# Attention LayerNorm rows of tiles 14 to 31 transposed on VectorE and by DMA, with channel blocks innermost, on one Trainium2 core

## The chip, the core and the metric

The kernel runs on one core of one Trainium2 chip. The core has TensorE (PE, matrix products into PSUM; its weight loads are shown as PEld), VectorE (DVE), ScalarE (ACT), GpSimd (POOL) and SyncE (SP, which issues all DMAs here). The metric is the device time in microseconds, the median of several runs. Before the change it is 463.86 us (three runs, 463.34 to 464.38).

## What is computed

A sequence of 2048 rows with 512 channels passes twice through an attention layer and an MLP layer with the same weights. Each has a LayerNorm ahead of it and a residual behind it. Attention has 32 heads of 16 channels and a sliding window of 256 rows.

```python
def _A_ref(x, wqkv, wo):
    B, S, D = x.shape
    H = 32; Dh = D // H; W = 256
    qkv = (x @ wqkv).reshape(B, S, 3, H, Dh).transpose(2, 0, 3, 1, 4)
    q, k, v = qkv[0], qkv[1], qkv[2]
    scores = jnp.einsum("bhqd,bhkd->bhqk", q, k) * (Dh ** -0.5)
    idx = jnp.arange(S)
    mask = (idx[:, None] - idx[None, :] >= 0) & (idx[:, None] - idx[None, :] < W)
    scores = jnp.where(mask[None, None], scores, -1e9)
    p = _softmax(scores, axis=-1)
    o = jnp.einsum("bhqk,bhkd->bhqd", p, v)
    return o.transpose(0, 2, 1, 3).reshape(B, S, D) @ wo

def _B_ref(x, w1, b1, w2, b2):
    h = _gelu(jnp.einsum("bsd,df->bsf", x, w1) + b1)     # 512 -> 1792
    return jnp.einsum("bsf,fd->bsd", h, w2) + b2         # 1792 -> 512

x = A_x
x = x + _A_ref(_layernorm(x, axis=-1), A_wqkv, A_wo)
x = x + _B_ref(_layernorm(x, axis=-1), B_w1, B_b1, B_w2, B_b2)
x = x + _A_ref(_layernorm(x, axis=-1), A_wqkv, A_wo)
x = x + _B_ref(_layernorm(x, axis=-1), B_w1, B_b1, B_w2, B_b2)
```

## The kernel before

Rows are worked on in tiles of 128. The two passes have 16 tiles each and are numbered through as tiles (tau) 0 to 31, so attention tile 16 reads the rows that MLP tile 0 of the first pass wrote. Two tiles make an attention batch, 16 batches in all. X, all weights and every intermediate stay in SBUF; input and weights are loaded in the first 40 us, and the only other traffic is the scratch transposes described below and the output.

For a batch b, `lnq(b)` normalizes two tiles (`layernorm`, layer 0), brings them channel-major into `xnTA[:, b % 2]` and projects Q from it; `kv(b)` projects K and V from the same buffer (`proj`, `pe_group`). Q and K use `xnTA` as the moving operand, 256 columns in each of the four channel chunks dc; V uses it as the stationary operand, 128 columns per tile and chunk. `xnTA` has two buffers, so batch b+2 can be written only when Q, K and V of batch b have read it. `attention(b)` then makes score visits (24 or 16 small matmuls into four PSUM banks, an exponential of ScalarE for each two banks, line 1111, and 0/1 masks on VectorE or GpSimd, line 1132), the product with V into two banks (PV), and the division, transposed on VectorE (lines 1197 to 1207). `outproj` adds the output projection to X (`residual`, line 990), and `layernorm(tau, 1, ...)` prepares the MLP's operand `xnTB`. `mlp(J)` runs jobs of two or four tiles: W1, GELU on ScalarE into `gT`, W2, residual.

`layernorm` has statistics and normalization on VectorE and GpSimd (lines 933 to 943), which give `xn`, rows in partitions. Then there are two ways to put channels in partitions. The first: four 128x128 transposes on TensorE into one PSUM bank (line 36 is the helper that records them) and one copy out of PSUM by VectorE (line 916) or ScalarE (line 918). The second, taken where `by_dma(tau, layer)` holds: VectorE transposes each 32x32 block within its 32 partitions (line 952, into the buffer `xs_`), four DMAs write one 32-row group each into the scratch `scr` in HBM (line 956), and one DMA reads it back with 1 KB in each partition (line 960). Before the change this second way is taken by MLP tiles 4 to 29 and by no attention tile.

PSUM has eight banks. A group takes banks from the first free entry of its class's list: "sc" four banks for a visit, "od" two for PV, "o" and "m1" one. The class "o" holds Q, K, V, output projection, W2, the first six W1 groups of a job and the transposes; its list is banks 6 and 7.

All instructions are added as nodes with what they read and write. The sequence on every engine is a written-out list of node numbers, `ORDER`; a negative entry ~i means node i on its second engine (a copy on ScalarE for VectorE, a mask or a product on GpSimd). `_Plan.follow` walks the list and assigns banks by estimated times; each engine then runs its part of the list strictly in order, with semaphore waits where data or buffers require them. SyncE's queue is one such sequence: a DMA whose data or target are not ready holds up the DMAs behind it.

Of the kernel before, what the change touches and what calls it, by code (L numbers as in the profile page):

```python
# [6 lines left out]
dt = mybir.dt  # L7
# [511 lines left out]
def bass_interleave_layers__sliding_block__dense_activation_gelu__prompt_kernel(  # L519
# [11 lines left out]
    Bb, S, D = A_x.shape  # L531
    assert Bb == 1
    P = 128
# [28 lines left out]
    NXS = 3  # L562
    NSC = 4

    def by_dma(tau, layer):
        return layer and 4 <= tau < NT - 2
# [26 lines left out]
    with ExitStack() as kctx:  # L593
        S_ = _Sched(nc, kctx)

        def sb(name, shape, dtype=dt.bfloat16):
# [21 lines left out]
        scr = nc.dram_tensor("scr_x", (NSC, 4, 32, 4, P), dt.bfloat16, kind="Internal").ap()  # L618
        xnTA = sb("xnTA", [P, 2, DC, 2 * P])
# [16 lines left out]
            3, 0, 8, 9, 10, 4, 5, 6, 7, 18, 19, 20, 21, 22, 15, 23, 33, 24, 40, 34, 41, 1, 11, 12, 13, 14, 2, 35, 36,  # L636
            42, 43, 84, 85, 86, 37, 44, 16, 17, 38, -40, 77, 45, -47, 87, 88, 89, -91, 57, 58, 59, 47, 60, 78, 79, 80,
            81, 82, -84, 48, 49, 52, 50, -52, 25, 91, 92, 93, 94, -96, 26, 53, 54, 55, -57, 72, 61, 154, 155, 156, 96,
            62, 63, 64, 67, 65, 68, 69, 70, 97, -72, 145, 146, 98, 99, 73, 74, 75, -101, 236, 101, 237, 108, 102, 103,
            229, 109, 110, 104, 105, 111, 66, 358, 359, 238, 230, 360, 361, 76, 135, 136, 137, 112, 231, 138, 139, 147,  # L640
            -149, 232, 239, 365, 28, 158, 159, 27, 140, 141, 142, 106, 107, 143, -145, 29, 30, 149, 150, 151, -158,
            -154, 815, 31, 32, 366, 367, 113, 114, 587, 594, 125, 126, 127, 160, 115, 116, 117, 118, 119, 163, 164,
            165, 128, 129, 120, 121, 122, 123, 124, 183, 184, 185, 253, 254, 255, 130, 256, 131, 240, 166, 233, 257,
            187, 189, 188, -162, -153, -163, 368, 132, 133, 134, 234, 235, 588, 951, 178, 180, 179, 263, 264, 241, 242,
            265, 266, 267, 192, 194, 193, 362, 369, 595, 243, 244, 245, 246, 247, -192, 958, 167, 182, 190, 248, 249,
            250, 251, -253, 168, 169, 170, 959, 589, 258, 259, 260, 261, 262, 172, 268, 269, 270, 271, -273, -197, 186,
            181, 173, 174, 363, -365, 286, 287, 288, 590, -172, 370, 371, 175, 273, 274, 275, 195, 197, 198, 176, 822,
            177, 291, 292, 293, 372, 373, 374, 375, -291, -277, 199, 200, -202, 378, 277, 278, 279, -295, -296, 376,
            377, 379, 380, 381, 382, 202, 383, 282, 284, 283, 384, 385, 386, 387, 823, 388, 816, -281, 216, 311, 313,
            312, 217, 218, 219, 203, 204, 205, 206, 281, 289, 220, 315, 316, 317, -286, 300, 207, 596, 208, 209, 210,  # L650
            296, 298, 297, 221, 222, 211, 212, 223, 301, 302, 320, 321, 322, 213, 224, 225, 226, 404, 406, 405, 214,
            817, 227, 430, 960, 431, 416, 417, 591, 299, 303, 432, -320, -326, 961, 215, 418, 306, 308, 307, 413, 414,
            415, 420, 421, 422, 389, 408, 410, 409, 427, 428, 429, 419, 433, 439, 440, 464, 465, 466, 467, 468, 441,
            390, 434, 435, 436, 437, 391, 423, 424, 392, 309, 318, 310, 314, 323, 326, 425, 426, 324, 411, 438, 469,
            470, 471, 327, 472, 473, 393, -305, 328, 454, 444, 459, 460, 461, 462, 442, 455, 456, 597, 598, 329, 330,
            331, 463, 443, 445, 446, 447, 448, 457, 458, 449, 450, 399, 451, 452, 453, 518, 400, 401, 519, 520, 402,
            403, 394, 395, 396, 397, 398, 952, 489, 490, 491, 492, 305, 824, 592, 593, 504, 505, 506, 493, 494, 332,
            333, 334, 335, 336, 337, 338, 495, -413, 228, 825, -408, -522, 339, 340, 508, 509, 496, 497, 345, 346, 347,
            348, 349, 350, 507, 513, 351, 352, 510, -512, 515, 514, -517, 353, 498, 499, 500, 501, 502, 503, 1216, 474,
            533, 535, 534, 475, 476, 477, 478, 479, 480, 528, 530, 529, 599, 600, 341, 354, 1217, 512, 517, 1218, 481,  # L660
            482, 483, 484, 485, 953, 342, 343, -537, -532, 537, 538, 539, -542, -541, 818, 486, 487, 488, 1209, 522,
            355, -357, 523, 524, 542, 543, 544, -547, -546, 671, 672, 673, 657, 658, 659, 525, 640, 642, 641, 664, 665,
            666, 668, 669, 670, 654, 644, 646, 645, 655, 1210, 656, 601, 602, 603, 604, 605, 532, 826, 526, 1211, 819,
            527, 661, 635, 636, -648, 637, -640, 662, 663, 606, 607, 547, 608, 609, -611, 548, 549, 550, 649, 650, 651,
            616, 617, 618, 619, 620, 611, 612, 631, 632, 613, 614, 615, 667, 680, 681, 682, 683, 684, 690, 691, 675,
            676, 692, 705, 693, 694, 677, 678, 679, 674, 685, 686, 687, 688, 689, 706, 707, 708, 709, -552, 552, 570,
            571, 572, 573, 574, 575, -649, -644, 357, -654, 954, 1212, 344, 700, 701, 660, 702, 703, 704, 553, 554,
            555, 556, 557, 558, 559, 560, 576, 577, 561, -653, 621, 710, 695, 696, 697, 698, 699, 711, 712, 622, 713,
            714, 623, 624, 625, 626, 627, 628, 629, 630, 764, 578, 820, 821, 715, 716, 827, 717, 828, 718, 719, 720,
            829, 830, 831, 633, 638, 955, 634, 562, 563, 567, 566, 962, 579, 580, 581, 583, 582, 564, 565, 584, 585,  # L670
            568, 766, 765, -770, 755, 756, 757, -760, 749, 750, 751, 752, 753, 754, 832, -834, 770, 772, 771, -775,
            -774, 721, 722, 723, 724, 725, 726, 745, 746, 747, 834, 835, 836, 837, 838, 727, 728, 729, 1345, 748, 758,
            760, 762, 761, 763, 767, 730, 731, 732, 733, 734, 863, 1219, 586, -769, 735, 736, 737, 738, 739, 775, 776,
            777, 778, -780, 864, 865, -868, 877, 878, 879, -882, 849, 740, 850, 741, 742, 743, 744, 868, 869, 870,
            -872, 851, 852, 853, 780, 839, 840, 841, 842, 843, 859, 861, 860, -867, -863, 844, 845, 846, 847, 848, 901,
            902, 903, -906, 854, 855, 856, 857, 858, 781, 782, 783, 784, 785, 786, 872, 874, 798, 799, 800, 801, 802,
            787, 956, 957, 873, 876, 875, 788, 892, 894, 893, 975, 976, 963, 964, 1346, 880, 803, 789, 804, 805, 790,
            791, 793, 794, 792, 977, 978, 897, 899, 898, 965, 966, 882, 884, 883, 967, 886, 968, -970, 887, 806, 807,
            808, 795, 810, 812, 809, 811, 896, 979, -905, 797, -901, -896, -886, 1004, 1006, 1005, 888, 1352, 889, 970,
            995, 996, 997, 980, 981, 982, 983, 906, 907, 908, 984, 910, 909, 1353, 971, 972, 973, -975, 1008, 1010,  # L680
            1009, 796, 813, 1043, 1044, 1045, 1213, 890, 891, 911, 1046, 1047, 1048, 999, 1001, 1000, -1003, -1004,
            1060, 1061, 1062, 1050, 912, 913, 1033, 1035, 1034, 1051, 1052, 914, -916, -1012, 985, 986, 987, 988, 989,
            1018, 1020, 1019, -1008, -1013, 990, 991, 992, 993, 994, 1053, 1013, 1014, 1015, -999, 916, 1054, 1055,
            1233, 1234, 1235, 1236, 1237, 1028, 1030, 1029, 917, 918, 919, 920, 921, 922, 1354, 1220, 1016, 934, 935,
            936, 1017, 1038, 1040, 1039, 1057, 1058, 1059, 1056, 1094, 1049, 1095, 1096, 1022, 1097, 1098, 1063, -1033,
            923, 924, 925, 926, 927, 937, 938, 939, 1021, 1037, 1031, 940, 941, 1214, 1215, 1064, 1099, 1100, 1023,
            1065, 1069, 1070, 1074, 1066, 1067, 1068, 1075, 1076, 1077, 1078, 942, 569, 1024, 1025, -1027, 1347, 1348,
            1027, 943, 944, 945, 930, 947, 948, 946, 949, 1071, 1072, 1073, 1101, 1102, 1089, 1079, 1080, 1090, 1081,
            1091, 1103, 1082, 1083, 1092, 1084, 1085, 1093, 1086, 1087, 1088, 1266, 1268, 1355, -1043, 1267, -1271,
            933, 814, 1104, 1105, 1106, 1149, 1150, 1107, 1108, 1109, 1151, 1152, 1153, 1154, 1155, 1253, 1254, 1255,  # L690
# [302 lines left out]
        def lnq(b, prio, pair=(0, 0)):  # L993

            xs = b % 2
            for j in range(2):
                layernorm(2 * b + j, 0, xnTA[:, xs, :, j * P : (j + 1) * P].rearrange("p c (r j) -> p r c j", r=4), "xa%d_%d" % (xs, j),
                          prio + (60 * j if b < 2 else 0))
# [360 lines left out]
```

## Time and profile before

| What | us |
|---|---|
| median of three runs | 463.86 |
| the profiled execution | 463.21 |
| its span, first to last instruction | 461.5 |
| TensorE busy | 435.0 |
| ScalarE busy | 393.2 |
| VectorE busy | 353.9 |
| GpSimd busy | 266.2 |
| Q and K matmuls (128x256, 512 of them), mean of one | 0.277 |
| one TensorE transpose, mean of one | 0.220 |

The granted TensorE clock is 0.996 of full speed. Durations of matmuls include their latency, which the next matmul overlaps; where it matters, the distance between the starts of two matmuls is used. DMA engines are busy for 13.5% of the span on average, most of it in the first 40 us. In lines of the profile, "out<-in" names what is written and read, and the numbers after the bar are busy time, mean duration in ns, and the idle time before those instructions with what ended it.

### The profile page before, as it was taken

The page shows a single profiled execution, that of the slowest core. Times are in us where ns is not written, and L with a number is a line of the kernel's source. Part 1 is how long each engine was busy: PE and PEld are TensorE (multiplying, and loading weights), DVE is VectorE, ACT ScalarE, POOL GpSimd, SP SyncE. Part 2 cuts the span into 40 slices and gives each one's busy share as a digit, 9 for nine tenths or more (in the row PEclk, how much of TensorE's full clock was granted, in tenths as well). Part 3 has the DMA queues.
Part 4 walks back from the last instruction along what each step waited for, and adds up shares of the span by engine and source line. Part 5 has one row for each costly group of instructions (what it writes and reads, how often), then busy time and mean ns, then how long its engine had stood idle before and what let it go on. Part 6 is the DMA issues. An engine that isn't in the chain of part 4 may idle for free.

```text
span 461.5 us, 19303 instructions
## 1 busy us (share of the span) xinstructions
PE 435.0 (94%) x8723; PEld 235.2 (51%) x8793; DVE 353.9 (77%) x699; ACT 393.2 (85%) x474; POOL 266.2 (58%) x302
## 2 busy tenths in 40 slices
PE   7997799999879999999999999999999999999997
PEld 3554464654444455555445545555454554454663
DVE  5998887887978679886998789885877867586402
ACT  3998999998999979898997999979988899873342
POOL 4367446776647466784629677595527535763210
PEclk9998999999999999999999999999999999999999
DMA  7570000002020011102010012101010111002101
GB/s 228 194 277 4 4 3 3 4 6 46 3 48 3 14 26 18 46 7 44 15 37 4 4 20 46 31 12 38 6 45 14 31 43 41 21 6 58 58 11 59
DMA packets 27857, 18.18 MB, mean 39 GB/s; under 512 B 15869, under 2 KB 27261, under 8 KB 27773
## 3 DMA queue, kind: packets, MB, share of 16 engines
q1 hardware_dynamic: 27772, 16.92, 13.5%
q8 instruction: 69, 1.13, 1.0%
q14 instruction: 16, 0.12, 0.1%
HBM read 11.41 MB, written 5.51 MB: 37 GB/s over the span
## 4 chain that ended last, share of the span: by engine, by line
PE 71%; ACT 16%; DVE 6%; DMA 2%; issue 2%; POOL 1%; SPq 1%; DVEq 0%; POOLq 0%
PE ps L32 69%; ACT E L1111 12%; PE ps L36 2%; SPq L956 1%; ACT gT L1278 1%; DMA scr_x<-xs_ 1%; DMA xnTB<-scr_x 1%; POOL E L1132 1%; DVE X L990 1%; ACT gT L1269 1%; DVE gT L1266 1%; DVE stat L933 1%; DVE xs_ L952 1%; ACT L1111 1%; ACT L1269 1%
## 5 line engine op out<-in xcount | busy, mean ns | idle before, releaser
L1111 ACT ACTIVATE E<-ps 128x1024 bf16<-128x1024 f32 x304 | 286.6, 1051 | 25.9 <-PE ps L32 25.1
L1132 POOL TENSOR_TENSOR E<-E,mask 128x512 bf16<-128x512 bf16 (+1 forms) x170 | 174.6, 1047 | 104.9 <-ACT E L1111 39.9
L32 PE MATMUL ps<-xnTB,W_sb 128*128 128x512 bf16 (+1 forms) x560 | 113.1, 337 | 0.9 <-DMA xnTB<-scr_x 0.6
L32 PE MATMUL ps<-W_sb,gT 128*128 128x512 bf16 x409 | 105.9, 380 | 4.7 <-issue 3.4
L990 DVE TENSOR_TENSOR X<-X,ps 128x512 bf16<-128x512 bf16 x64 | 43.5, 682 | 41.3 <-PE ps L32 40.7
L32 PEld LDWEIGHTS ps<-xnTB,W_sb 128*128 128x128 bf16 x560 | 50.5, 98 | 45.4 <-issue 2.0
L32 PE MATMUL ps<-QT,KT 32*64 32x320 bf16 (+4 forms) x2976 | 65.1, 259 | 7.5 <-ACT E L1111 4.3
L32 PE MATMUL ps<-xnTA,Wqkv_sb 128*128 128x256 bf16 x512 | 70.4, 277 | 1.1 <-ACT E L1111 0.5
L1278 ACT ACTIVATE gT<-ps,b1T 128x512 bf16<-128x512 f32 (+1 forms) x92 | 48.1, 587 | 24.2 <-PE ps L32 23.7
L32 PEld LDWEIGHTS ps<-W_sb,gT 128*128 128x128 bf16 x448 | 39.2, 98 | 45.1 <-issue 5.5
L940 POOL TENSOR_TENSOR rstd<-veps,mhalf 128x1 f32<-128x1 f32 x64 | 36.0, 566 | 42.9 <-DVE veps L937 41.6
L32 PEld LDWEIGHTS ps<-xnTA,Wqkv_sb 128*128 128x128 bf16 x512 | 45.9, 99 | 20.2 <-issue 4.0
L32 PEld LDWEIGHTS ps<-QT,KT 32*64 32x64 bf16 x2976 | 27.3, 103 | 51.5 <-ACT E L1111 38.4
L32 PE MATMUL ps<-E,Va 64*17 64x128 bf16 (+3 forms) x3872 | 49.1, 229 | 1.6 <-POOL E L1132 0.4
L32 PEld LDWEIGHTS ps<-E,Va 64*17 64x17 bf16 x3872 | 39.4, 85 | 19.5 <-PE ps L32 7.2
L1030 DVE TENSOR_TENSOR KT<-ps,parmask 128x1024 bf16<-128x1024 f32 x32 | 38.6, 1213 | 10.9 <-PE ps L32 10.6
L1197 DVE STREAM_TRANSPOSE TT<-ps 128x1024 f32<-128x1024 f32 x32 | 39.8, 1245 | 8.8 <-PE ps L32 7.6
L933 DVE BATCH_NORM_STATS2 stat<-X 128x6 f32<-128x512 bf16 x64 | 43.8, 689 | 2.0 <-DMA X<-in_A_x_dram 0.8
L1266 DVE TENSOR_SCALAR gT<-ps,b1T 128x512 bf16<-128x512 f32 (+1 forms) x48 | 31.8, 672 | 15.2 <-PE ps L32 14.7
L1241 POOL TENSOR_TENSOR X<-X,b2b 128x512 bf16<-128x512 bf16 x32 | 36.7, 1153 | 4.7 <-DVE xn L943 3.2
L1132 DVE TENSOR_TENSOR E<-E,mask 128x512 bf16<-128x512 bf16 (+1 forms) x92 | 34.8, 412 | 5.8 <-ACT E L1111 5.8
L32 PE MATMUL ps<-Wqkv_sb,xnTA 128*128 128x512 bf16 x110 | 30.1, 380 | 2.2 <-issue 0.8
(49 smaller groups left out, 322.3 us busy)
## 6 DMA issues: line engine op xcount, KB each, us to landing
W_sb<-in_B_w_dram SPq DMA_DIRECT2D x2, 1792.0 KB, 12.9
scr_x<-xs_ SPq DMA_DIRECT2D x104, 32.0 KB, 1.7
xnTB<-scr_x SPq DMA_DIRECT2D x26, 128.0 KB, 2.1
out_dram<-X SPq DMA_DIRECT2D x16, 128.0 KB, 1.8
Wqkv_sb<-in_A_wqkv_dram SPq DMA_DIRECT2D x3, 512.0 KB, 6.7
X<-in_A_x_dram SPq DMA_DIRECT2D x3, 512.0 KB, 4.8
X<-in_A_x_dram SPq DMA_DIRECT2D x2, 256.0 KB, 2.9
Wo_sb<-in_A_wo_dram SPq DMA_DIRECT2D x1, 512.0 KB, 6.6
```

The costliest lines, as they stand in the source:

```text
L32: return self.e.matmul(*a, **k)
L36: return self.e.transpose(*a, **k)
L933: add("dve", lambda e, B: e.bn_stats(stat6[:, k6, :], X[:, t, :]), 590, reads=["X%d" % t], writes=["st%d" % k6], prio=prio)
L940: add("pool", lambda e, B: e.tensor_tensor(out=rstd[:, k : k + 1], in0=veps[:, k : k + 1], in1=mhalf[:], op=ALU.pow), 535, reads=["ve%d" % ...
L990: add("dve", lambda e, B: e.tensor_tensor(out=X[:, t, :], in0=X[:, t, :], in1=ps[:, B[g][0], :], op=ALU.add), d_psum(512), reads=["X%d" % ...
L1030: add("dve", lambda e, B, g=g, i=i: e.tensor_tensor(out=KT[:, kb, :, 2 * i : 2 * i + 2, :].rearrange("p a c q -> p a (c q)"), in0=ps[:, B[ ...
L1111: add("act", lambda e, B, g_=g_, gi=gi: e.activation(E[:, 2 * gi : 2 * gi + 2, e0 : e0 + 512], ps[:, B[g_][0] : B[g_][0] + 2, :], AF.Exp, ...
L1132: op = lambda e, B, Ew=Ew, Mw=Mw: e.tensor_tensor(out=Ew, in0=Ew, in1=Mw, op=ALU.mult)
L1197: add("dve", lambda e, B: e.transpose(TT[:, s].rearrange("p a c q d -> p (a c q d)"), ps[:, B[g][0] : B[g][0] + 2, :].rearrange("p a n -> ...
L1241: add("pool", lambda e, B: e.tensor_tensor(out=X[:, t, :], in0=X[:, t, :], in1=b2b[:], op=ALU.add), 1110, reads=["X%d" % t, "b2b"], writes ...
L1266: add("dve", lambda e, B, g=g, fc=fc: e.tensor_scalar(out=gT[:, fc, 0:M], in0=ps[:, B[g][0], 0:M], scalar1=b1T[:, fc : fc + 1], scalar2=No ...
L1278: add("act", lambda e, B, g=g, fc=fc: e.activation(gT[:, fc, 0:M], ps[:, B[g][0], 0:M], AF.Gelu_apprx_tanh, bias=b1T[:, fc : fc + 1], scal ...
```

## The change

- `by_dma` also holds for attention tiles 14 to 31. Their rows go through VectorE's block transpose, four scatter DMAs and one load, in place of four TensorE transposes and one copy out of PSUM.
- `xnTA` changes from [128, 2, 4 chunks, 256 rows] to [128, 2, 256 rows, 4 chunks]: the chunk is the innermost index, for all 32 attention tiles. A matmul that reads one chunk steps over four elements. The 14 tiles that stay with TensorE write their copy with that step too.
- `xs_` gets a fourth slot, used by attention tiles alone; the scratch gets 16 places for attention tiles and 16 for MLP tiles, in place of four in all.
- The list of the class "o" has all eight banks, each alone.
- `ORDER` is a new list throughout, with 3367 entries for 3295.

```diff
-    NXS = 3
-    NSC = 4
+    NXS = 4
+    NSC = 16
 
     def by_dma(tau, layer):
-        return layer and 4 <= tau < NT - 2
+        return 4 <= tau < NT - 2 if layer else tau >= 14
...
-        scr = nc.dram_tensor("scr_x", (NSC, 4, 32, 4, P), dt.bfloat16, kind="Internal").ap()
-        xnTA = sb("xnTA", [P, 2, DC, 2 * P])
+        scr = nc.dram_tensor("scr_x", (2 * NSC, 4, 32, 4, P), dt.bfloat16, kind="Internal").ap()
+        xnTA = sb("xnTA", [P, 2, 2 * P, DC])
...
-            "o": [(6,), (7,)],
+            "o": [(6,), (7,), (5,), (4,), (3,), (2,), (1,), (0,)],
...
-        xs_rr = [0]
+        xs_rr = [0, 0]
...
             if by_dma(tau, layer):
-                z = xs_rr[0] % NXS
-                v = xs_rr[0] % NSC
-                xs_rr[0] += 1
+                z = xs_rr[1] % (NXS - 1) if layer else NXS - 1
+                v = xs_rr[layer] % NSC + (0 if layer else NSC)
+                xs_rr[layer] += 1
                 add("dve", lambda e, B: e.transpose(
-                    xs_[:, z, :].rearrange("p (q d j) -> p d q j", q=4, d=DC), xn[:, s, :].rearrange("p (d q j) -> p d q j", q=4, d=DC)), 630,
+                    xs_[:, z, :].rearrange("p (q d j) -> p d q j" if layer else "p (q j d) -> p d q j", q=4, d=DC), xn[:, s, :].rearrange("p (d q j) -> p d q j", q=4, d=DC)), 630,
...
-                dma(lambda e, B: e.dma_start(dst.rearrange("p r d j -> p (r d j)"), scr[v].rearrange("q i r c -> (q i) (r c)")),
+                dma(lambda e, B: e.dma_start(dst.rearrange("p r d j -> p (r d j)" if layer else "p r d j -> p (r j d)"), scr[v].rearrange("q i r c -> (q i) (r c)")),
...
-                layernorm(2 * b + j, 0, xnTA[:, xs, :, j * P : (j + 1) * P].rearrange("p c (r j) -> p r c j", r=4), "xa%d_%d" % (xs, j),
+                layernorm(2 * b + j, 0, xnTA[:, xs, j * P : (j + 1) * P].rearrange("p (r j) c -> p r c j", r=4), "xa%d_%d" % (xs, j),
...
-                pe_group(g, [(Wqkv_sb[:, dc, which * D + kc * P : which * D + (kc + 1) * P], xnTA[:, xs, dc, :],
+                pe_group(g, [(Wqkv_sb[:, dc, which * D + kc * P : which * D + (kc + 1) * P], xnTA[:, xs, :, dc],
...
-                pe_group(g, [(xnTA[:, xs, dc, j * P : (j + 1) * P], Wqkv_sb[:, dc, 2 * D : 3 * D], slice(0, 512),
+                pe_group(g, [(xnTA[:, xs, j * P : (j + 1) * P, dc], Wqkv_sb[:, dc, 2 * D : 3 * D], slice(0, 512),
```

## The prediction

> **What bounds the kernel now.** I read the page's busy times, then the chain of waits, then busy time by stretch, then single stretches of the timeline.
>
> ```profile
> span 461.5 us, 19303 instructions
> PE 435.0 (94%) x8723; PEld 235.2 (51%) x8793; DVE 353.9 (77%) x699; ACT 393.2 (85%) x474; POOL 266.2 (58%) x302
> ...
> PE 71%; ACT 16%; DVE 6%; DMA 2%; issue 2%; POOL 1%; SPq 1%; DVEq 0%; POOLq 0%
> ```
>
> TensorE is idle for 461.5 - 435.0 = 26.5 us, and the chain that ended last runs through it for 71%. Busy time is modelled, so it is checked against stretches:
>
> ```profile
> 0.00:60.00 60.00, 50.06 (x948) 30.18 (x954) 50.34 (x122) 49.76 (x59) 32.74 (x51) 0.97 0.41 136
> ...
> 0.00:120.00 120.00, 107.50 (x2302) 63.27 (x2324) 99.93 (x219) 107.81 (x133) 74.36 (x95) 0.99 0.23 74
> 120.00:340.00 220.00, 211.99 (x4489) 110.38 (x4531) 181.02 (x353) 201.76 (x232) 138.15 (x149) 1.00 0.11 23
> 340.00:461.50 121.50, 115.51 (x1949) 61.59 (x1968) 72.91 (x129) 83.66 (x110) 53.68 (x59) 1.00 0.13 35
> ...
> 440.00:461.50 21.50, 18.41 (x113) 10.96 (x114) 2.75 (x4) 7.49 (x18) 0.00 (x0) 1.00 0.11 38
> ```
>
> The columns are the stretch, its length, then PE, PEld, DVE, ACT, POOL busy. In the first 60 us TensorE idles 9.9 us (loads, then exponentials), in the last 21.5 us 3.1. Between 60 and 440 us 13.4 us are left. From 120 to 340 us, where every transpose of tiles 14 to 31 lies, it idles 8.0 of 220 us, ScalarE 18 and VectorE 39. So work taken from TensorE there should shorten the span, unless ScalarE (92% busy) sets the pace.
>
> **What the change takes from TensorE.** Tiles 14 to 31 are 18 tiles of four 128x128 transposes, 72 of the 152:
>
> ```profile
> 149.68 0.39 PE L32 MATMUL ps<-xnTB,W_sb 128*128 128x512 bf16 x1
> 150.12 0.39 PE L36 MATMUL ps<-ident,xn 128*128 128x128 bf16 x4
> 150.34 0.81 PE L32 MATMUL ps<-xnTB,W_sb 128*128 128x512 bf16 x3
> 151.09 0.80 PE L32 MATMUL ps<-E,Va 64*17 64x256 bf16 x64
> ```
>
> Four transposes occupy the array from 150.12 to 150.34, 0.22 us start to start; their 0.39 is latency that the next matmul overlaps. 18 x 0.22 = **4.0 us**. The last two lines price something else: three 512-column matmuls last 3 x 0.216 = 0.65 us (the W_sb,gT stream runs at 0.216 each), so the PV block could start at 150.99 and starts at 151.09: a change of the kind of tile (full array, 32-row scores, 64x17 PV) costs 0.10 us. The order is a list of node numbers, in the sequence of the add calls; with the 18 x (6 - 2) = 72 added nodes the new list has 3367 against 3295, and naming each entry shows 387 such changes on TensorE before and 374 after. 13 x 0.10 = **1.3 us**. Matmul counts stay otherwise.
>
> **What it adds elsewhere.**
>
> ```profile
> L952 DVE STREAM_TRANSPOSE xs_<-xn 128x512 bf16<-128x512 bf16 x26 | 18.2, 703 | 0.6
> L916 DVE COPY xnTA<-ps 128x512 bf16<-128x512 bf16 x19 | 7.8, 412 | 1.6 <-PE ps L36 1.6
> L918 ACT ACTIVATE xnTA<-ps 128x512 bf16<-128x512 bf16 x13 | 7.7, 598 | 8.0 <-PE ps L36 7.9
> L916 DVE CAST Va<-ps 128x512 bf16<-128x512 f32 x23 | 15.3, 673 | 1.5 <-PE ps L32 1.3
> L1132 POOL TENSOR_TENSOR E<-E,mask 128x512 bf16<-128x512 bf16 x133 | 150.8, 1152 | 97.0 <-ACT E L1111 34.9 <-DVE E L1132 25.7 <-DVE TM L1202 19.9
> ```
>
> The last line is from the listing that keeps forms apart. VectorE gains 18 x 0.703 = 12.7 us. By the new order 39 masks come to it from GpSimd: 30 double ones at 0.423 and 9 single ones at 0.284 (VectorE's own rows of these forms), 15.2 us, and GpSimd loses 30 x 1.152 + 9 x 0.670 = 40.6. Copies into xnTA on VectorE go from 19 to 11 (-3.3), five Q evacuations go to ScalarE (-5 x 0.685), one V evacuation and one TM product come back (+0.7 each). The 11 remaining copies now write every fourth element. No row shows that; bounds are the present 412 ns and the 673 ns of the CAST, and I take 673, because packed writing is lost: +2.9. Sum: 353.9 + 12.7 + 15.2 - 3.3 - 3.4 + 1.4 + 2.9 = 379 us, 83% of the new span. ScalarE: 393.2 - 10 x 0.598 + 5 x 0.628 - 0.608 = 390. Neither passes TensorE's 435 - 5.3 = 430.
>
> [...]
>
> **The added DMAs.** 72 scatters and 18 loads go into SyncE's queue, among the 104 + 26 of the MLP tiles.
>
> ```profile
> scr_x<-xs_ SPq DMA_DIRECT2D x104, 32.0 KB, 1.7
> xnTB<-scr_x SPq DMA_DIRECT2D x26, 128.0 KB, 2.1
> ```
>
> An issue occupies the queue 0.43 us (chain, 126.46 to 128.84), so 90 take 39 us of a queue that the 130 fill for 56. From xn to xnTA the path was about 0.9 us (transposes with latency 0.39, copy 0.41, hand-over) and becomes 0.70 + 4 x 0.43 + 1.7 + 0.34 + 2.1 = 6.6. Whether that shows depends on the order. Counting the TensorE work (0.216 us for a 512-column matmul, 0.109 for 256, 0.36 a score visit, 0.74 a PV block, 0.10 a change of kind) that the new list puts between a tile's load entry and the first Q matmul reading it gives 3.2 us (tile 28) to 22 us; issue and landing need 2.4. The one xs_ slot of these tiles is reused 2.2 us of such work or more after the last scatter's entry, against 1.7 landing. A load also waits until the buffer's last reader is done; tiles 14, 18, 19 and 22 are listed 0.6 to 0.9 us behind it, and MLP scatters queue behind them, but these have 2 us or more to spare. So I cost the DMAs at nothing; if the cover were gone, each of the nine pairs could be 5.7 us late, 51 us in all. The same path for the 26 MLP tiles now makes TensorE itself wait 0.6 us in all.
>
> **The strided reads.** All 512 Q and K matmuls now stream xnTA at every fourth element, and 128 V matmuls load weights so. The trace has no such read; the nearest rows are equal to each other (xnTB in runs of 32 elements and gT contiguous both 380 ns at 128x512). Bounds: nothing, or half speed, 256 x 0.42 ns = 107 ns for each of the 512, 55 us. I take nothing, as the broken runs of xnTB cost nothing. The V weight loads (98 ns) lie under 216 ns matmuls even if doubled.
>
> **Idle time.** Any of eight banks for single groups, against two, removes waits, and the knot from 119.8 to 134 us (residual, statistics, two xnTA copies and the first MLP scatter in the chain) loses its copies: the order puts the VectorE transposes of tiles 14 and 15 some 13 us of TensorE work or more before their use. The stretch 120 to 140 idles 3.6 us; I take half back, -1.8. Against it, TensorE's waits put down to VectorE, without the start, are 4.5 us; they grow by 7% if they follow VectorE's busy time and by 45% if they follow its busy to idle ratio: I take +0.8. Net **-1.0**, bounds -13.4 (all of it) and +4.5 (VectorE's waits doubled).
>
> **Sum.** 461.5 - 4.0 - 1.3 - 1.0 = 455.2 us of span. The profiled execution took 463.21, 1.7 more than its span, and the median of 463.86 is 0.65 above that: **457.6 us**. The likeliest case's own range is 453 to 462.
>
> **Rivals.**
> 1. *More than the work* (0.15). Bank choice and order take most of the 13.4 us of inner idle: 450 to 453 and a little below. For: TensorE's in-order stops are short and many. Against: ScalarE at 92% from 120 to 340 us.
> 2. *The transposes were hidden* (0.12). If ScalarE's exponentials set the pace there, the 4.0 us become idle: 463.86 - 1.3 = 462.6, or up to 464.8. For: weight loads wait 42.7 us for E. Against: of those waits only 5.3 us reach TensorE itself. The change would then not do what it says.
> 3. *Strided streaming slows Q and K* (0.14), the slower side. One mechanism: it decides from 6.3 us / 512 = 12 ns per 256-column matmul. At 20 ns the time is 457.6 + 10 = 468, at half speed 512. Nothing in the profile speaks for it, nothing excludes it. [...]
> 4. *The DMA path arrives late* (0.09). Each of nine pairs late by over 6.3 / 9 = 0.7 us decides; the margin of tile 28 is 3.2 - 2.4 = 0.8, so 1 to 1.5 us each gives 460 to 464 plus what queues behind: 465 to 472.
>
> **Numbers.** The forecast has 0.50. About 0.2% (0.9 us) can be told from no change. Faster: 0.50 + 0.15 + 0.05 of the second rival = 0.70; same 0.07; slower 0.14 + 0.09 = 0.23. The range 450 to 468 leaves out some 0.06 below and 0.12 above.
>
> **What would show it.** 80 transposes left on TensorE; TensorE busy near 430 and idle near 25; Q and K matmuls still 273 to 277 ns, and 0.109 us start to start (any more is rival 3); xnTA copies near 673 ns; VectorE near 379, GpSimd near 225; TensorE waits for xnTA<-scr_x under 2 us (more is rival 4); TensorE idle from 120 to 340 us grown by 4 is rival 2. The prediction is wrong if the span falls or rises by more than TensorE's work and the idle bounds allow.

## The result and the profile after

| | before | after |
|---|---|---|
| median, us | 463.57 (462.08 to 464.38, 6 runs) | 521.89 (520.88 to 524.90, 6 runs) |
| profiled span, us | 461.5 | 520.3 |
| TensorE busy, us | 435.0 | 499.5 |
| Q and K matmul, mean ns | 277 | 403 |
| VectorE / ScalarE / GpSimd busy, us | 353.9 / 393.2 / 266.2 | 390.1 / 400.0 / 228.1 |

The ratio is 1.127, 95% interval [1.1248, 1.1295]: 58 us slower, where 457.6 us was forecast and 450 to 468 was the range.

The page of the changed kernel, with the same parts as before (busy time by engine, the chain that ended last, two of the costliest groups, the new load; line numbers are four higher than before):

```profile
span 520.3 us, 19365 instructions
PE 499.5 (96%) x8721; PEld 243.0 (47%) x8721; DVE 390.1 (75%) x745; ACT 400.0 (77%) x470; POOL 228.1 (44%) x262
...
PE 85%; DVE 6%; ACT 4%; SPq 1%; DMA 1%; issue 1%; POOL 0%; DVEq 0%; POOLq 0%
...
L32 PE MATMUL ps<-xnTA,Wqkv_sb 128*128 128x256 bf16 x512 | 128.9, 403 | 3.0 <-DVE xnTA L920 1.3
...
L956 DVE STREAM_TRANSPOSE xs_<-xn 128x512 bf16<-128x512 bf16 x44 | 41.5, 956 | 0.5
...
xnTA<-scr_x SPq DMA_DIRECT2D x18, 128.0 KB, 2.2
```

TensorE works more, 499.5 us for 435.0, and its share of the chain rises from 71 to 85%. One group stands out, Q and K, whose 512 matmuls last 403 ns instead of 277; its row before was:

```profile
L32 PE MATMUL ps<-xnTA,Wqkv_sb 128*128 128x256 bf16 x512 | 70.4, 277 | 1.1 <-ACT E L1111 0.5 <-DVE X L990 0.2
```

The load into xnTA lands in 2.2 us, where 2.1 was costed. The listing that keeps forms apart shows who else touches the new layout:

```profile
L920 DVE COPY xnTA<-ps 128x512 bf16<-128x512 bf16 x11 | 13.9, 1298 | 2.8 <-PE ps L36 2.8
L36 PE MATMUL ps<-ident,xn 128*128 128x128 bf16 x80 | 7.6, 224 | 2.1 <-ACT xnTA L922 1.3 <-ACT E L1115 0.5 <-DVE xnTA L920 0.4
L922 ACT ACTIVATE xnTA<-ps 128x512 bf16<-128x512 bf16 x3 | 3.8, 1339 | 10.6 <-PE ps L36 10.6
```

The writes with a step of four have become slow: copies 412 to 1298 ns on VectorE and 598 to 1339 on ScalarE. The 44 block transposes average 956 ns where 26 averaged 703, so the 18 new ones take (41.5 - 26 x 0.70) / 18 = 1.29 us each. 80 TensorE transposes are left, as forecast.

Durations hold latency, so the price of a Q or K matmul is read from the distance of starts. The timeline of the changed kernel (start, length, work):

```profile
31.82 2.89 PE L32 MATMUL ps<-xnTA,Wqkv_sb 128*128 128x256 bf16 x12
34.64 0.42 PE L32 MATMUL ps<-QT,KT 32*64 32x256 bf16 x16
```

Twelve take 2.89 us; without the last one's duration (0.405) that is 2.49 / 11 = 0.226 us from start to start. The kernel e9_all_packed below, the same but with packed reads and writes, has at this place:

```profile
31.02 1.48 PE L32 MATMUL ps<-xnTA,Wqkv_sb 128*128 128x256 bf16 x12
32.44 0.42 PE L32 MATMUL ps<-QT,KT 32*64 32x320 bf16 x16
```

(1.48 - 0.274) / 11 = 0.110 us. 512 x (0.226 - 0.110) = **59 us** of TensorE's time, about as much as the whole loss. The experiments show that the two are not the same: some of the 59 us fills idle time, and the slow writes cost time of their own. By stretch (length, then PE, PEld, DVE, ACT, POOL busy, clock) and by waits of TensorE (us, times, longest):

```profile
0.00:60.00 60.00, 51.10 (x601) 23.97 (x602) 42.63 (x89) 35.61 (x40) 21.24 (x40) 0.92 0.40 135
...
120.00:340.00 220.00, 215.06 (x4104) 99.34 (x4103) 180.51 (x337) 183.44 (x206) 102.51 (x112) 0.99 0.18 37
```

```profile
PE ps L32 <- ACT E L1115: 4.3, 12, 0.8
PE ps L32 <- DVE xnTA L920: 3.9, 5, 1.2
...
PE ps L32 <- DMA xnTA<-scr_x: 0.4, 1, 0.4
```

601 matmuls are done in the first 60 us, against 948 before, in as much busy time (51.1 us for 50.1): the loss begins with tiles that use no DMA. TensorE waits 0.4 us for loads into xnTA; for VectorE's copies it waits 3.9, against 0.9 before.

### The profile page after: what moved, and what is told of

Read it like the earlier page. It is cut to its first block, busy times and chain, and to the rows that moved or that the text cites. A ratio compares the mean times of both kernels' runs of the same rounds, so it can differ in the third digit from the quotient of the medians.

```text
span 520.3 us, 19365 instructions
## 1 busy us (share of the span) xinstructions
PE 499.5 (96%) x8721; PEld 243.0 (47%) x8721; DVE 390.1 (75%) x745; ACT 400.0 (77%) x470; POOL 228.1 (44%) x262
## 4 chain that ended last, share of the span: by engine, by line
PE 85%; DVE 6%; ACT 4%; SPq 1%; DMA 1%; issue 1%; POOL 0%; DVEq 0%; POOLq 0%
PE ps L32 85%; ACT E L1115 3%; DVE xnTA L920 2%; DVE X L994 1%; DMA xnTA<-scr_x 1%; DVE xs_ L956 1%; DVE TT L1201 1%; DVE E L1136 1%; SPq L960 1%; SPq L964 0%; DVE KT L1034 0%; ACT xnTA L922 0%; PE ps L36 0%; DMA xnTB<-scr_x 0%; DVE Va L920 0%
## 5 line engine op out<-in xcount | busy, mean ns | idle before, releaser
L1115 ACT ACTIVATE E<-ps 128x1024 bf16<-128x1024 f32 x304 | 290.2, 1033 | 62.3 <-PE ps L32 61.6
L1136 POOL TENSOR_TENSOR E<-E,mask 128x512 bf16<-128x512 bf16 (+1 forms) x131 | 135.5, 1051 | 135.9 <-DVE E L1136 55.2
L32 PE MATMUL ps<-xnTA,Wqkv_sb 128*128 128x256 bf16 x512 | 128.9, 403 | 3.0 <-DVE xnTA L920 1.3
L32 PE MATMUL ps<-W_sb,gT 128*128 128x512 bf16 x448 | 119.2, 381 | 0.8 <-DVE xnTA L920 0.5
L32 PE MATMUL ps<-xnTB,W_sb 128*128 128x512 bf16 (+1 forms) x560 | 116.1, 337 | 0.2 <-ACT E L1115 0.2
L32 PEld LDWEIGHTS ps<-xnTA,Wqkv_sb 128*128 128x128 bf16 x512 | 53.1, 111 | 58.1 <-issue 5.8
L32 PE MATMUL ps<-QT,KT 32*64 32x320 bf16 (+4 forms) x2976 | 66.4, 263 | 6.3 <-ACT E L1115 3.8
L1282 ACT ACTIVATE gT<-ps,b1T 128x512 bf16<-128x512 f32 (+1 forms) x92 | 48.9, 584 | 26.8 <-PE ps L32 26.3
L1136 DVE TENSOR_TENSOR E<-E,mask 128x512 bf16<-128x512 bf16 (+1 forms) x131 | 51.2, 418 | 5.4 <-ACT E L1115 5.1
L956 DVE STREAM_TRANSPOSE xs_<-xn 128x512 bf16<-128x512 bf16 x44 | 41.5, 956 | 0.5
L32 PE MATMUL ps<-Wqkv_sb,xnTA 128*128 128x512 bf16 x128 | 36.6, 385 | 0.0
```

The costliest lines, as they stand in the source:

```text
L32: return self.e.matmul(*a, **k)
L956: add("dve", lambda e, B: e.transpose(xs_[:, z, :].rearrange("p (q d j) -> p d q j" if layer else "p (q j d) -> p d q j", q=4, d=DC), xn[: ...
L1115: add("act", lambda e, B, g_=g_, gi=gi: e.activation(E[:, 2 * gi : 2 * gi + 2, e0 : e0 + 512], ps[:, B[g_][0] : B[g_][0] + 2, :], AF.Exp, ...
L1136: op = lambda e, B, Ew=Ew, Mw=Mw: e.tensor_tensor(out=Ew, in0=Ew, in1=Mw, op=ALU.mult)
L1282: add("act", lambda e, B, g=g, fc=fc: e.activation(gT[:, fc, 0:M], ps[:, B[g][0], 0:M], AF.Gelu_apprx_tanh, bias=b1T[:, fc : fc + 1], scal ...
```

## The experiments

Times are medians where there are several runs; ratios are to the kernel before, run on the same chip beside it (463.1 to 463.8 us).

### Reads, writes or DMAs?

**e2_inner_only**: the kernel before, with the layout alone changed.

```diff
-xnTA = sb("xnTA", [P, 2, DC, 2 * P])
+xnTA = sb("xnTA", [P, 2, 2 * P, DC])
```

> Before, with the channel chunk innermost in xnTA and nothing else (old order, two banks, all 32 attention tiles transposed on TensorE). Theory 1: 463.6 + 58 for the strided streams, and up to 32 x 0.8 = 26 us of longer copies, some of it hidden: 522 to 540. Rival A (order or DMA path): 464 to 470. Rival B (strided writes): 470 to 490, with Q and K matmuls at their old distance.

532.91 us (one run): 69 us slower with no new DMA, order or bank. So the layout alone is enough. Its rows:

```profile
L32 PE MATMUL ps<-xnTA,Wqkv_sb 128*128 128x256 bf16 x512 | 128.6, 403 | 3.4 <-ACT xnTA L918 1.3 <-DVE xnTA L916 1.3 <-DVE statmv L935 0.2
L916 DVE COPY xnTA<-ps 128x512 bf16<-128x512 bf16 x19 | 24.5, 1289 | 1.9 <-PE ps L36 1.9
L918 ACT ACTIVATE xnTA<-ps 128x512 bf16<-128x512 bf16 x13 | 16.8, 1334 | 12.7 <-PE ps L36 12.6
```

Q and K take the same 403 ns as after the change.

**e3_read_packed, e4_write_packed, e9_all_packed**: the changed kernel with its DMAs, order and banks, where Q and K read 256 neighbours (e3), where copies, block transposes and loads write runs (e4), or both and V's weights too (e9). The excerpt shows Q's and K's reads and the block transposes; copies and loads are altered in the same way.

```diff
 e3, e9: FL = xnTA[:, xs].rearrange("p n c -> p (n c)")
-xnTA[:, xs, :, dc]
+FL[:, dc * 256 : dc * 256 + 256]
 e4, e9: the block transposes
-"p (q d j) -> p d q j" if layer else "p (q j d) -> p d q j"
+"p (q d j) -> p d q j"
```

> After, with the Q and K matmuls reading 256 neighbouring elements of the same buffer in place of every fourth (so Q and K are made of other values than the reference's); the writes and the V weight loads keep their step of four. Theory 1: 521.9 - 58 = 464, between 458 and 468. Rival A: within 5 us of 522. Rival B (strided writes): 505 to 522.

> After, with the copies into xnTA and the block transposes writing neighbouring elements (so xnTA holds its values in another arrangement than the matmuls read, and the result differs from the reference's); all reads keep their step of four. Theory 1: the strided streams stay, 512 to 521 us, copies back at 0.41 us and block transposes at 0.70 us. Rival A: within 5 us of 522, too, told apart by the run with packed reads. Rival B: under 490.

> After, with neither reads nor writes at a step of four: Q and K stream 256 neighbouring elements, V loads 128 neighbouring weights, copies and block transposes write packed (so the values are arranged otherwise than the reference needs); order, banks and DMAs as in after, with the DMAs' old piece sizes. Theory 1 (the step of four is all that lost time, the rest does what was forecast): 454 to 460 us. Rival A, weaker form (the new order with its DMA path loses some 8 us by itself, as the 466 us with 64-byte pieces could also mean): 464 to 470, with waits of TensorE for xnTA<-scr_x or for VectorE of 4 us or more.

| reads / writes | us | span | TensorE busy | idle | granted clock |
|---|---|---|---|---|---|
| step 4 / step 4 (the change) | 521.89 | 520.3 | 499.5 | 20.8 | 0.984 |
| step 4 / packed (e4, one run) | 512.28 | 510.6 | 495.7 | 14.9 | 0.997 |
| packed / step 4 (e3, one run) | 474.44 | 472.7 | 443.4 | 29.3 | 0.993 |
| packed / packed (e9, 12 runs) | 461.88 | 462.3 | 439.7 | 22.6 | 0.999 |

The reads are worth 47.5 us (from the change to e3) to 50.4 (from e4 to e9), the writes 9.6 (from the change to e4) to 12.5 (from e3 to e9), together 60.0. V's packed weights are in the 50.4 and the 12.5. e2 and e4 lie in the ranges of theory 1. e3 lies 6 us above its range, which held nothing for the slow writes, and e9 2 us above its own: some 2 us are lost to something other than the step of four. (e9's profiled run, 464.01 us, is the longest of its 12, so its idle time is some 2 us above that of its median.) Rows of e4, then of e3:

```profile
L32 PE MATMUL ps<-xnTA,Wqkv_sb 128*128 128x256 bf16 x512 | 128.9, 403 | 0.9 <-ACT E L1115 0.5 <-issue 0.4
L956 DVE STREAM_TRANSPOSE xs_<-xn 128x512 bf16<-128x512 bf16 x44 | 30.5, 700 | 0.5
L920 DVE COPY xnTA<-ps 128x512 bf16<-128x512 bf16 x11 | 4.5, 414 | 1.0 <-PE ps L36 1.0
```

```profile
L32 PE MATMUL ps<-xnTA,Wqkv_sb 128*128 128x256 bf16 x512 | 71.9, 279 | 5.5 <-DVE xnTA L920 2.0 <-ACT E L1115 1.2 <-ACT xnTA L922 1.2
L956 DVE STREAM_TRANSPOSE xs_<-xn 128x512 bf16<-128x512 bf16 x44 | 41.5, 956 | 0.5
L920 DVE COPY xnTA<-ps 128x512 bf16<-128x512 bf16 x11 | 13.9, 1299 | 1.0 <-PE ps L36 1.0
```

Each slow row follows its own step alone. With slow reads, TensorE's busy time grows by 56 us and its idle time falls by 8 (e9 to e4): the others have longer to be ready, and ScalarE's exponentials wait 56.7 us for TensorE in e4 against 29.0 in e9. The slow writes come back as idle time, 6.7 us more of it (e9 to e3), of which half is waits for VectorE's copies (3.8 us put down to L920), and as 3.7 us of busy time. The granted clock is lower in both pairs that price the writes (0.993 for 0.999, 0.984 for 0.997); what that costs is in their price and isn't separated.

e9 keeps every DMA and is 0.9972 [0.9953, 0.9991] of before. So the DMA path isn't what made the change slow.

### What decides the price of a step

**e5_read_step2, e13_read_step3, e14_read_step8**: the changed kernel, with the step of Q's and K's reads alone altered.

```diff
-xnTA[:, xs, :, dc]
+FL[:, dc // 2 * 512 + dc % 2 : dc // 2 * 512 + 512 : 2]
+FL[:, dc * 64 : dc * 64 + 768 : 3]
+xnTA[:, xs].rearrange("p (m a) c -> p m (a c)", a=2)[:, None, :, dc].to_broadcast([P, 2, P])
```

> After, with the Q and K matmuls reading every second element of the same buffer (other values than the reference's; writes and V loads keep their step of four). If any step over one halves the stream: matmuls 0.224 us apart, within 6 us of 522. If the speed follows the elements taken from 16 bytes (four here, two in after): 0.111 us apart and near the 474 us of the run with packed reads; something between would be 0.15 to 0.18 apart and 490 to 505.

> After, with the Q and K matmuls reading every third element of the same buffer (other values than the reference's; writes and V loads keep their step of four). At a step of two 256 columns were 0.114 us apart, at four 0.226. If a stream needs the next 16 bytes no faster than a fixed pace, and this pace allows 8 bytes' worth of step per two columns, a step of three costs three quarters of step four: 0.165 to 0.175 apart, 495 to 502 us. If only steps that do not divide evenly or exceed two fall to half speed: 0.22 to 0.23, 517 to 524.

> After, with the Q and K matmuls reading 128 elements at a step of eight, twice, in place of 256 at a step of four (other values than the reference's; the rest as in after). If the pace is fixed per 16 bytes: a quarter of full speed, 0.43 to 0.46 us apart, 512 x 0.22 = 113 us over after, 630 to 640. If half speed is the floor for any wide step: 0.22 to 0.23, 517 to 526.

Twelve matmuls in a row, one line of the timeline from each, at steps of 2, 3 and 8:

```profile
37.23 1.53 PE L32 MATMUL ps<-xnTA,Wqkv_sb 128*128 128x256 bf16 x12
```

```profile
41.57 2.23 PE L32 MATMUL ps<-xnTA,Wqkv_sb 128*128 128x256 bf16 x12
```

```profile
45.66 5.58 PE L32 MATMUL ps<-xnTA,Wqkv_sb 128*128 128x256 bf16 x12
```

| step, bf16 elements | 1 | 2 | 3 | 4 | 8 |
|---|---|---|---|---|---|
| median of one, us | 0.273 | 0.275 | 0.335 | 0.405 | 0.631 |
| start to start, us | 0.110 | 0.114 | 0.172 | 0.226 | 0.450 |
| the kernel's time, us | 474.44 | 476.97 | 498.31 | 521.89 | 673.18 |

At the steps measured from 2 on, the time goes with the span that is read: 0.450 us for 256 elements 16 bytes apart is 1.76 ns per 16 bytes, and this gives 0.113, 0.169 and 0.225 at 2, 3 and 4, where 0.114, 0.172 and 0.226 were measured. At a step of 1 it would be 0.056, and the 0.110 measured with packed reads is longer. So a step of 2 is nearly free here (0.114 for 0.110) and 4 costs double (0.226). (The times of steps 1, 2, 3 and 8 are of one run each, all with the slow writes.)

At a step of 4 the pace doesn't follow the granted clock. From 46.5 to 49.8 us of the changed kernel the granted clock is 0.50, and twelve matmuls there take the same 2.89 us as the twelve above from 31.82, at a clock of 1.00:

```profile
47.20 2.89 PE L32 MATMUL ps<-xnTA,Wqkv_sb 128*128 128x256 bf16 x12
```

Packed reads do follow the clock: from 40.0 to 43.4 us of the kernel before, at 0.50, Q and K matmuls start 0.213 us apart in place of 0.109. Whether the pace goes by lines of 16 bytes or by bytes is not shown.

e5 and e13 lie where a pace per 16 bytes had put them. e14 misses its expected time (630 to 640) by 33 us though its matmuls are as expected. The busy time by stretch shows a granted clock of 0.69 and 0.71 for the first 120 us:

```profile
0.00:60.00 60.00, 54.57 (x276) 16.72 (x279) 26.31 (x60) 22.21 (x24) 16.46 (x35) 0.69 0.43 134
60.00:120.00 60.00, 54.52 (x829) 22.16 (x832) 37.02 (x77) 35.59 (x44) 14.99 (x16) 0.71 0.01 2
```

Twelve matmuls at a step of 8 take 5.58 us from 45.66, in a slice of e14's page at a clock of 0.7, and 5.59 from 71.42, in one at 0.5; matmuls with packed reads take longer at 0.50 (0.213 for 0.109 us, above). That can account for the miss; it wasn't taken apart. What slows the clock is open.

### Can the rows be had packed?

Three layouts that give the reference's result. **e1_outer** keeps the chunk outermost, as before the change, so the scatters write 64-byte pieces for 256-byte ones. **e12_step2** has two halves of 256 rows by 2 chunks, and 128-byte pieces. **e11_runs** lays xnTA out in runs of 32 like xnTB; V's weights, which then have no single step, come in four tiles of 128x32. The excerpt shows the layout and, for e1 and e12, the order in the scratch.

```diff
+e1:  [P, 2, DC, 2 * P]        scr "(e i r j) -> r i e j", e=16
+e12: [P, 2, 2, 2 * P, 2]      scr "(e i r f) -> r i e f", e=8
+e11: [P, 2, 2, 4, DC, 32]     V: 4 x matmul(ps[32 * q : 32 * q + 32, ...], xnTA[:, xs, j, q, dc, :], ...)
```

> After, with the channel chunk outermost in xnTA again (256 neighbouring elements per chunk, as before the change); order, any bank and the transposes of attention tiles 14 to 31 by VectorE and DMA stay (the scatters write 64-byte pieces, the load reads 256-byte pieces). Theory 1 (the Q and K matmuls stream every fourth element at half speed, 512 x 0.114 = 58 us, and little else is lost): 521.9 - 58 - a few us for the copies and block transposes that write packed again, 455 to 462 us, Q and K matmuls 0.109 to 0.111 us apart. Rival A (order or DMA path is what lost the time): over 470. Rival B (strided writes of copies and block transposes lose most): also near 460, but then the run with packed writes alone is near it too.

> After, with xnTA as two halves of 256 rows x 2 chunks: every read of a chunk steps over two elements, scatters write 128-byte pieces and loads read 512-byte pieces, and the result is the reference's. From the run with reads at a step of two (0.111 us apart) the streams are at full speed. If copies and block transposes at a step of two cost 0.41 and 0.70 us: 460 to 465 us; if 1.3 us as at a step of four: 468 to 475.

> After, with xnTA laid out as xnTB (row group, chunk, 32 rows), so that copies, block transposes and the 1 KB loads are packed and Q and K stream in runs of 32; the V weights, which then have no single step, are loaded as four tiles of 128x32 with one 512-column matmul each, side by side in the array. It computes the reference's result. If the four run at the same time as the 64x17 tiles of PV do: 455 to 462 us by theory 1, 464 to 470 by rival A. If they run one after another: 128 x 3 x 0.216 = 83 us more, near 540.

| | us | ratio to before |
|---|---|---|
| e1_outer (12 runs) | 466.15 | 1.0058 [1.0031, 1.0085] |
| e12_step2 (5 runs) | 465.88 | 1.0043 [1.0031, 1.0056] |
| e11_runs (6 runs) | 474.80 | 1.0259 [1.0231, 1.0287] |

All three undo most of the loss, and none is below the kernel before. e1 and e12 fall between the ranges that were expected, e11 outside all of its own. e1's TensorE waits 4.4 us for loads from the scratch (1.8 of it for xnTA), e9's 2.2. e12 still reads at a step of 2 (0.004 x 512 = 2 us). In e11 the planner's estimates had put 160 of 657 groups on other banks, so it was run again with the changed kernel's banks: **e15_runs_pinned**.

> The layout of e11 (Q, K and the DMA pieces as in xnTB's packed runs, V in four 128x32 column tiles), the reference's result, with every group of matmuls on the bank that it has in the changed kernel. If e11's 474.8 us came from the 160 groups that its estimates had put on other banks, this takes 460 to 464, like e9_all_packed (461.9). If V's extra matmuls and weight loads cost it, 470 to 476 as before, and the idle time of TensorE stays near e9's 22.6 us while its busy time is above 445.

469.38 us, 1.0128 [1.0102, 1.0154]; TensorE busy 447.4, idle 21.8. So V's form costs 7.5 us against e9, all of it busy time (447.4 against 439.7), and the banks had cost 5.4. Four 128x32 tiles run side by side: sixteen fill the array from 97.28 to 98.26 where e9 has four full ones from 95.92 to 96.88. The price is the change of the kind of tile: one such set takes 0.33 us to the next start, one full matmul 0.22 (e15, then e9), and with V's tiles as a kind of their own the order has 63 changes more, 63 x 0.11 = 6.9 us:

```profile
99.71 0.40 PE L32 MATMUL ps<-Wqkv_sb,xnTA 128*32 128x512 bf16 x4
100.04 0.39 PE L32 MATMUL ps<-W_sb,gT 128*128 128x512 bf16 x1
```

```profile
98.12 0.38 PE L32 MATMUL ps<-Wqkv_sb,xnTA 128*128 128x512 bf16 x1
98.34 0.38 PE L32 MATMUL ps<-W_sb,gT 128*128 128x512 bf16 x1
```

### What order, banks and DMAs are worth without the layout

**e6_any_bank** is the kernel before with the list of eight banks for "o". **e10_old_order_dma** has the DMA path and packed steps in the order of before. **e8_no_dma** is the changed kernel's order with 17 of the 18 tiles (all but 28) transposed on TensorE, in the old layout; **e16_no_dma_pinned** repeats it with the changed kernel's banks, since e8 had got others for 168 groups. **before_again** is the kernel before.

```diff
 e6, against the kernel before
-            "o": [(6,), (7,)],
+            "o": [(6,), (7,), (5,), (4,), (3,), (2,), (1,), (0,)],
 e8, e16, against the changed kernel (without the changes of layout and order)
-        return 4 <= tau < NT - 2 if layer else tau >= 14
+        return 4 <= tau < NT - 2 if layer else tau in (28,)
```

> Before, with eight banks in the list of the class o and nothing else. The forecast put a part of its 1.0 us of idle time here: 461 to 464 us by it. Rival: bank choice alone takes several us: under 460.

> Before's order and two banks, with attention tiles 14 to 31 transposed by VectorE and DMA, all steps packed (values arranged otherwise than the reference needs): the block transpose and its scatters stand where the TensorE transposes stood, the load where the copy stood. The old order leaves 1 to 24 us from transpose to first reader, 5 us or less for 13 of the 18 tiles, and the path needs 6.6. Theory: each pair with too little lead is 2 to 5 us late, 8 of 9 pairs: 475 to 500 us, TensorE waiting for xnTA<-scr_x for 15 us or more. Rival: the waits are filled by work of the order that follows: 459 to 466.

> After's order, banks and masks, with the chunk outermost in xnTA again and attention tiles 14 to 31 (without 28, which stays with the DMAs, in 64-byte pieces) transposed on TensorE and copied by VectorE at the place of the order where the buffer is free. To be held against 461.9 us, the run of after with all steps packed. If the transposes on TensorE lie on the path at the forecast price: 17 x 0.22 = 3.7 us more, 465 to 467. If the DMA path costs about what it saves: 461 to 463. If it costs more: under 461.

> The changed kernel's order with all steps packed, and the 17 tiles that took the path over block transposes and DMAs transposed on TensorE instead; all groups that both have keep the changed kernel's banks. Held against e9_all_packed (461.9 us), whose 17 tiles take that path. If taking 68 transposes off TensorE is worth the forecast 17 x 0.22 = 3.7 us, this takes 464.5 to 467. If the path by VectorE and DMA gives its gain back in waits, 460.5 to 463. If e8's 476.1 had nothing to do with its 168 other banks, 474 to 477.

> Before, unchanged, for a second trace: the first holds 8723 TensorE matmul records for 8793 weight loads, and the run of before with eight banks, which has all 8793, shows 444.2 us of TensorE busy time where the first trace of before shows 435.0. If the 70 missing records made idle time that was none: TensorE busy 442 to 446 us with all records, idle 16 to 20 us in place of 26.5. If not: 435 and 26 again.

| | us | ratio to before | TensorE busy, idle |
|---|---|---|---|
| e6_any_bank (5 runs) | 473.31 | 1.0222 [1.0196, 1.0247] | 444.2, 26.3 |
| e10_old_order_dma (4 runs) | 546.11 | 1.1779 [1.1757, 1.1802] | 451.4, 92.9 (records missing, below) |
| e8_no_dma (5 runs) | 476.10 | 1.0273 [1.0252, 1.0294] | 435.1, 39.5 (records missing, below) |
| e16_no_dma_pinned (5 runs) | 471.34 | 1.0163 [1.0138, 1.0188] | 444.5, 25.1 |
| before_again (one run) | 464.35 | | 435.4, 27.2 (records missing, below) |

e6: any bank, in the old order, costs 10 us. 311 of 675 groups get another bank, and the waits of TensorE for exponentials, which hold the other banks, go from 5.3 to 12.0 us. Counting on a gain was wrong here. The new order with two banks wasn't tried: its list has more than two of these groups open at a time.

e10: without the new order the loads come late, and the kernel takes longer than the 475 to 500 us that were expected. TensorE's longest wait by far:

```profile
PE ps L32 <- DMA xnTA<-scr_x: 56.7, 7, 11.9
```

The price named for the lost cover was 51 us. The other 25 of the 82 us over the kernel before aren't taken apart: 169 groups had other banks as well, and the granted clock was 0.93.

e16: against e9, the 68 transposes cost 444.5 - 439.7 = 4.8 us of TensorE's time and 2.5 of idle, in which it waits 2.6 us for copies into xnTA; 9.5 us between the medians. That lies in none of the three ranges expected. So the path over VectorE and DMA is worth more than forecast, in this order. But the same order with TensorE's transposes is 7.8 us slower than before: e9's gain is the difference of the two. Some of those 7.8 may be the place I gave to the transposes in the list.

before_again was run to get the missing matmul records, and shows the same 70 too few, 8723 of 8793, as before; e8, e10, e12, e13 and e14 lack 70 to 76 too, the change, e1 to e6, e9, e11, e15 and e16 none. e1 and e12 do the same matmuls, e12's 2 us slower by their step: 439.8 us busy with all records, and 433.1 in place of some 441.8 with 75 missing. So before's 435.0 us is too low by an estimated 8 (8.7 x 70 / 75) to 9 us (e6 has its matmuls complete at 444.2), and its idle time is some 17 to 18 us, not 26.5.

## Why the prediction was wrong

**The step that failed** is the strided reads: "Bounds: nothing, or half speed, 256 x 0.42 ns = 107 ns for each of the 512, 55 us. I take nothing, as the broken runs of xnTB cost nothing." They cost 116 ns each, 59 us of TensorE's time, and 47.5 to 50.4 us of the kernel's. The mechanism was named, as the third rival, with 512 us at half speed and a chance of 0.14; it happened at slightly under half speed (0.226 us for 0.110). The row chosen to weigh the ends was not the near one: xnTB's runs of 32 elements are packed, so they span as many bytes per element as a contiguous read, and the row says nothing about a step. No other row of the trace had a step, which speaks for leaving the range open to both ends.

**The copies** were taken at 673 ns; they took 1298, and on ScalarE, where no loss was counted, 1339 for 598. The block transposes were taken at 703 and took 1290. In e12, at a step of two, copies take 724 and 742 ns, and all 44 block transposes 719 on average, which is some 745 for the 18 that write with the step. So a step of two does cost VectorE's copies time, 724 ns for 415, and that is near the price I took; a step of four costs nearly twice as much, 1298. VectorE ends at 390 against 379 forecast: 11 x 0.63 + 18 x 0.59 = 17.5 us for the writes, less 5 to 7 by which the rest of the sum was too high (e9, without slow writes: 371.4 us, where the forecast less its 2.9 for the copies is 376). ScalarE ends at 400 against 390; its three slow copies are 2 us of that, and e9 has 392. On the path these writes cost 9.6 to 12.5 us, where the forecast held nothing.

**The DMAs** at nothing: right. TensorE waits 0.4 us for loads into xnTA in the slowed kernel and not at all in e9, and GpSimd is at 228 us against 225. Without the new order they would show, as e10 does. Rival 4 didn't happen.

**The transposes** at -4.0 for 18 tiles: right in kind. 17 tiles are worth 4.8 us of busy time and 7.3 us of span between e16 and e9. Rival 2, in which they become idle time, is out for this order: the idle time falls too, from 25.1 to 22.6 us. **The changes of kind** at 0.10 us: e15 shows 0.11 at another pair of kinds; that 13 fewer give 1.3 us was not tested by itself.

**Idle time** at -1.0: wrong in sign, as far as the missing records let it be known. e9's idle time for its median (461.9 - 1.7 - 439.7) is 20.5 us, against some 17 to 18 before. TensorE's waits for exponentials are 7.5 us in e9 against 5.3 before, and those for loads into xnTB 2.2 against 0.6. The latter belong to the order and not to the new DMAs, since e16 has 2.0 with one attention tile on that path. Neither reason that was given for a gain held. A free choice of banks costs time where it was tried by itself (e6). And the knot from 120 to 140 us didn't dissolve with its copies: from 120 to 200 us TensorE idles 4.5 us in e9 and 4.9 before (with 11 of 1705 matmul records missing), and e9's chain still holds the MLP's load (2% of the span), the scatters' issues and the residual (1% each). The bounds had also been drawn from 26.5 us of idle time, of which 8 to 9 were work.

This is why the change without its slow steps reaches 461.9 and not 457.6: TensorE's work falls by an estimated 3.5 to 4.5 us (435.0 and 8 to 9, less 439.7) where 5.3 was forecast, and its idle time doesn't fall. How much of this is the choice of banks in the new order stays open.

The range missed because its upper end, 468, cut off a rival whose own price was 512, at a chance that came from the missing evidence and not from any against it.

## What to carry to other kernels

When a layout puts an index innermost, price every reader and writer of it, at its step: the change saved 72 TensorE transposes of 0.055 us and slowed 512 matmuls by 0.116. Here a step of two bf16 in what TensorE streams was nearly free (0.114 us for 0.110), three cost half as much again (0.172) and four double (0.226); where no row has the step, measure one before building on it. Compare the count of matmul records with that of weight loads before idle time is read as a reserve.

## What was not expected of the hardware

- Q's and K's matmuls stream at some 1.76 ns per 16 bytes spanned at steps of 2, 3, 4 and 8 (0.114, 0.172, 0.226 and 0.450 us for 256 columns). A step of 4 takes the same 0.226 us at a granted clock of 0.50 as at 1.00, while packed reads go from 0.109 to 0.213.
- V's weight loads hardly mind a step of four: they take 116 ns (e2, e3, e4) for 97 (e9), less than the 216 ns of the 512-column matmuls beside them.
- VectorE's 128x512 copies into xnTA take 415, 724 and 1298 ns at steps of 1, 2 and 4 (e9, e12, the change), ScalarE's 595, 742 and 1339: a step of four isn't cheap on ScalarE either.
- At a step of eight, in e14, the granted clock is 0.69 and 0.71 in the first two stretches of 60 us, though TensorE is shown busy for 54.5 us of each. A step of four alone doesn't do it: e4 has 1.00 in the first 60 us. The changed kernel's 0.92 there goes with 8.9 us of idle time.
- The choice of PSUM banks alone moved the time by 5 us twice (474.80 to 469.38 us from e11 to e15, 476.10 to 471.34 from e8 to e16), with the same work in the same order. 160 and 168 of the 657 groups moved, of which 90 and 94 are groups of one bank.
